# Where ScalarE reads the redo flag: moving a flag load and a branch ahead of the waits for the last stores

## The chip, the cores and the metric

The kernel runs on one core of one Trainium2 chip. Times are device microseconds (us) of that core. The profile's span goes from the first to the last instruction of the program; the device time is about 1.8 us longer.

## The reference, cut to what matters

```python
# x: (1, 384, 384, 384) bfloat16, w1d: (1,) bfloat16
g = jnp.einsum("bhwc->bc", x) / (H * W)      # mean of each channel
s = sigmoid(g * w1d[0])                      # k = 1: one weight
return x * s[:, None, None, :]               # scale each channel
```

The result needs a mean over all of x before the first value may be written. Reading x twice would cost half as much traffic again, so the kernel speculates. It computes a scale `s_early` from the first 135 of 1152 row groups, writes everything with that scale, and meanwhile sums the rest. At the end it computes the true scale, compares the two bit by bit, and repeats the whole pass only if they differ. With these inputs they do not differ.

## The kernel before

SyncE issues the loads of 26 tiles of 4.3 to 4.4 MB. TensorE sums them, VectorE multiplies them in place, ScalarE issues the 26 stores. `plan.final` is the list of the stores' semaphores and values.

```python
    # ... after the last tile: true scale, comparison, flag
    plan.op("scalar", lambda e: e.activation(s_true[:], total[:], ACT_F.Sigmoid, ...), ...)
    plan.op("vector", lambda e: e.tensor_tensor(total[:], s_true[:].bitcast(U16),
                                   s_early[:].bitcast(U16), ALU.not_equal), ...)
    plan.op("vector", lambda e: e.reduce_max(wrong[:], total[:], axis=mybir.AxisListType.X), ...)
    plan.op("vector", lambda e: e.tensor_copy(redo[:], wrong[:]), ...)
    checked = (plan.sems["vector"], plan.count["vector"])
    # ... `again` is the plan of the second pass
    stored = nc.alloc_semaphore("stored")

    with nc.Block() as block:

        def second_pass(name, e):
            e.wait_ge(*checked)
            flag = e.value_load(redo[0:1, 0:1], min_val=0, max_val=1)
            with e.If(flag > 0):
                if name != "scalar":
                    e.wait_ge(stored, 1)
                again.emit(name, e)

        # ... sync and vector: plan.emit(name, e); second_pass(name, e)

        @block.scalar
        def _(e):
            plan.emit("scalar", e)
            for token in plan.final:
                e.wait_ge(*token)
            e.sem_inc(stored, 1)
            second_pass("scalar", e)
        # ... tensor and gpsimd: plan.emit alone
```

A second pass must not overwrite output that a store of the first pass is still writing, so `stored` guards it. ScalarE therefore waits for all stores, gives `stored`, and only then loads the flag and branches. (A semaphore is a counter that one instruction raises and another waits for.) The block ends with a barrier: in the trace the last instruction of each other engine in the block, its drain, raises one semaphore; GpSimd waits until all have raised it, and then releases all with another.

## Time and profile before

| | before |
|---|---|
| device time, median of 3 runs (range) | 533.75 us (533.66 to 533.89) |
| span of the profiled run, which is not one of the three and took 534.2 us | 532.4 us |
| traffic | 113.25 MB read, 113.25 MB written |

These are the span line, the slices of the DMA engines, two queue lines and the total of the traffic from the page of the kernel before. One digit stands for a fortieth of the span; 9 means busy for 90% or more. A queue line gives packets, megabytes and the share of the 16 engines' time.

```profile
span 532.4 us, 2500 instructions
...
DMA  9999999999999999999999999999999999999995
...
q10 hardware_dynamic: 3746, 113.25, 49.3%
...
q14 instruction: 2, 0.02, 0.0%
...
HBM read 113.25 MB, written 113.25 MB: 425 GB/s over the span
```

The kernel is bound by the DMA engines in every slice but the last. There traffic runs out, and an instruction's latency can be seen in the time.

The chain of waits does not show that latency. It ends as follows (start in us, length in us, what):

```profile
504.64 0.57 DVE total L281
505.21 0.02 issue
505.24 0.56 DVE wrong L289
505.80 0.02 issue
505.82 0.15 DVE redo L295
```

The chain stops at 505.97 us, 26.4 us before the span's end, because it follows the engines' own work. After that there are only DMA transfers and instructions of the sequencers: waits, register loads, branches. The view of one source line shows these too. Below are lines 326 (flag load), 327 (branch), 346 (store waits), 347 (last wait with the increment) and 322 (closing drain and barrier) of before. "SPq" is SyncE's sequencer, the part of the engine that waits and branches; ACT is ScalarE, DVE VectorE and POOL GpSimd; after the count come minimum, median and maximum duration in ns, then the start of the first and of the last one in us.

```profile
L326 SPq TENSOR_LOAD <-redo x1: 832/832/832, 506.0 to 506.0; - x1
L326 DVEq TENSOR_LOAD <-redo x1: 932/932/932, 506.0 to 506.0; - x1
...
L326 ACTq TENSOR_LOAD <-redo x1: 475/475/475, 530.9 to 530.9; - x1
L326 ACTq FUSED_REGOPS  x1: 173/173/173, 531.4 to 531.4; - x1
L326 ACTq SEQ_ASSERT  x1: 18/18/18, 531.6 to 531.6; - x1
...
L327 ACTq COMPARE_BRANCH  x1: 54/54/54, 531.6 to 531.6; - x1
...
L346 ACTq EVENT_SEMAPHORE  x12: 38/38/38, 504.0 to 530.7; - x12
...
L347 ACTq EVENT_SEMAPHORE  x1: 38/38/38, 530.8 to 530.8; - x1
...
L322 POOLq EVENT_SEMAPHORE  x2: 17/17/17, 532.2 to 532.3; - x2
...
L322 SPq DRAIN  x1: 51/51/51, 507.7 to 507.7; - x1
...
L322 ACTq DRAIN  x1: 67/67/67, 532.1 to 532.1; - x1
```

SyncE and VectorE loaded the flag at 506.0 us; SyncE was in its drain at 507.7. ScalarE loaded it at 530.9. Its drain at 532.1 is what the barrier waited for. The same records with three decimals, for ScalarE and the barrier (start, duration, what; us):

```
530.712 0.038  ScalarE  wait that the last store ended (its 16th landing: 530.691)
530.789 0.038  ScalarE  wait (already met) and increment of `stored`
530.893 0.475  ScalarE  load of the flag
531.397 0.173  ScalarE  register operations
531.600 0.018  ScalarE  assert
531.647 0.054  ScalarE  compare and branch (taken)
532.135 0.067  ScalarE  drain
532.234 0.017  GpSimd   barrier: all have drained
532.312 0.017  GpSimd   barrier: release; the span ends at 532.417
```

I call the time from the start of the first of these lines to the span's end the **tail**: here 532.417 - 530.712 = 1.705 us. The start of a wait's record may be used as the moment at which the store was seen: the Trainium skill, "Perfetto Trace Analysis", section "Per-engine timelines", says that for an instruction run by the sequencer the profiler reports as start the moment when all its semaphores are satisfied. This trace agrees: the wait's record starts 21 ns after the last landing.

### The profile page before, as it was taken

Reading aid. Unit: us, or ns where it says so; the run is one execution under the profiler, and the core shown is the slowest. Engines: PE = TensorE matmul, PEld = TensorE weight load, DVE = VectorE, ACT = ScalarE, POOL = GpSimd, SP = SyncE. Lnnn points to the kernel's source line nnn. Section 1 sums busy time; section 2 is a strip of 40 time slices with the busy share of each in tenths; the row PEclk is TensorE's granted clock in tenths of the full one; section 3 lists DMA queues with packets and bytes.
Section 4 is the critical chain, followed back from the end, with each engine's and each line's share of the span. In section 5 each row is a group of like instructions: output and inputs, shape, how many; then the busy total and the mean of one; then the engine's idle time right before and its main releaser. Section 6 shows DMA issues by size and latency. Waiting matters only on the chain.

```text
span 532.4 us, 2500 instructions
## 1 busy us (share of the span) xinstructions
PE 243.2 (46%) x1153; PEld 127.8 (24%) x1153; DVE 236.7 (44%) x34; ACT 2.7 (1%) x4; POOL 0.3 (0%) x5
## 2 busy tenths in 40 slices
PE   0979643347156156266266156266265255165100
PEld 0435311123023033133133033033132133032000
DVE  0006999551642642633633642632633642633700
ACT  1000000000000000000000000000000000000000
POOL 0000000000000000000000000000000000000000
PEclk9989867587686786775676686786675686786755
DMA  9999999999999999999999999999999999999995
GB/s 371 418 450 421 411 415 454 418 449 417 447 416 449 414 448 425 434 442 423 432 444 424 432 443 421 434 444 415 439 444 421 434 440 424 434 442 423 432 440 241
DMA packets 7501, 226.66 MB, mean 426 GB/s; under 512 B 834, under 2 KB 834, under 8 KB 834
## 3 DMA queue, kind: packets, MB, share of 16 engines
q1 hardware_dynamic: 3744, 113.25, 49.6%
q10 hardware_dynamic: 3746, 113.25, 49.3%
q8 instruction: 9, 0.15, 0.1%
q14 instruction: 2, 0.02, 0.0%
HBM read 113.25 MB, written 113.25 MB: 425 GB/s over the span
## 4 chain that ended last, share of the span: by engine, by line
another core or an unknown queue 63%; DMA 20%; DVE 7%; PE 3%; SPq 1%; issue 1%; ACT 0%; DVEq 0%
DMA arena<-in_x_dram 12%; DMA out_dram<-arena 8%; DVE arena L165 7%; PE acc L206 3%; SPq L91 1%; ACT s_early L255 0%; ACT s_true L273 0%; DVE total L281 0%; DVE total L249 0%; DVE wrong L289 0%; DVE total L267 0%; SPq L99 0%; DVE redo L295 0%; DVEq L99 0%
## 5 line engine op out<-in xcount | busy, mean ns | idle before, releaser
L206 PE MATMUL acc<-arena,ones 128*128 128x384 bf16 x1152 | 243.0, 383 | 249.2 <-DMA arena<-in_x_dram 249.2
L165 DVE TENSOR_TENSOR arena<-arena,s_early 128x16896 bf16<-128x16896 bf16 (+1 forms) x26 | 234.1, 9019 | 224.3 <-PE acc L206 223.6
L206 PEld LDWEIGHTS acc<-arena,ones 128*128 128x128 bf16 x1152 | 127.7, 113 | 364.2 <-DMA arena<-in_x_dram 258.9
L249 DVE COPY total<-acc 128x384 f32<-128x384 f32 x1 | 0.6, 558 | 42.1 <-PE acc L206 42.1
L273 ACT ACTIVATE s_true<-total,w_scaled 128x384 bf16<-128x384 f32 x1 | 0.6, 615 | 458.2 <-DVE total L267 458.2
L177 ACT ACT_TABLE_LOAD x1 | 1.3, 1283 | 1.3 <-PEq L370 1.3
L183 PE MATMUL acc<-w_one,ones 1*128 1x1 bf16 x1 | 0.2, 158 | 2.0 <-DMA w_one<-in_w1d_dram 2.0
L281 DVE TENSOR_TENSOR total<-s_true,s_early 128x384 f32<-128x384 uint16 x1 | 0.6, 559 | 0.7 <-ACT s_true L273 0.7
L255 ACT ACTIVATE s_early<-total,w_scaled 128x384 bf16<-128x384 f32 x1 | 0.6, 616 | 42.4 <-DVE total L249 42.4
L192 DVE TENSOR_SCALAR w_scaled<-acc 128x1 f32<-128x1 f32 x2 | 0.2, 153 | 1.2 <-PE acc L183 1.2
L183 PEld LDWEIGHTS acc<-w_one,ones 1*128 1x128 bf16 x1 | 0.1, 99 | 2.0 <-issue 2.0
L289 DVE TENSOR_REDUCE wrong<-total 128x1 f32<-128x384 f32 x1 | 0.6, 553 | 0.0
L267 DVE TENSOR_TENSOR total<-total,acc 128x384 f32<-128x384 f32 x1 | 0.5, 546 | 0.0
L173 DVE MEMSET ones<- 128x128 bf16 x1 | 0.2, 165 | 0.8 <-PEq L370 0.8
L177 ACT ACTIVATE warm<-warm 128x1 f32<-128x1 f32 x1 | 0.2, 203 | 0.0
L295 DVE CAST redo<-wrong 128x1 int32<-128x1 f32 x1 | 0.2, 154 | 0.0
L370 POOL MEMSET const-bfloat16-1.0<- 128x1 bf16 x1 | 0.1, 102 | 0.0
L370 POOL MEMSET const-uint8-127<- 128x1 uint8 x1 | 0.1, 102 | 0.0
L172 POOL MEMSET warm<- 128x1 f32 x1 | 0.1, 99 | 0.3 <-POOLq L370 0.3
L370 POOL MEMSET const-float32-0.0<- 128x1 f32 x1 | 0.1, 99 | 0.2 <-issue 0.2
L370 POOL MEMSET const-float32-1.0<- 128x1 f32 x1 | 0.1, 99 | 0.0
## 6 DMA issues: line engine op xcount, KB each, us to landing
arena<-in_x_dram SPq DMA_DIRECT2D x18, 4224.0 KB, 28.9
out_dram<-arena ACTq DMA_DIRECT2D x18, 4224.0 KB, 72.2
arena<-in_x_dram SPq DMA_DIRECT2D x8, 4320.0 KB, 31.0
out_dram<-arena ACTq DMA_DIRECT2D x8, 4320.0 KB, 58.7
w_one<-in_w1d_dram ACTq DMA_DIRECT2D x1, 0.0 KB
```

Of the source, the lines that this page charges most:

```text
L91: ("op", lambda e: e.dma_start(out, in_), self.pool[i], 16)
L165: return lambda e: e.tensor_tensor(v, v, s_b, ALU.mult)
L177: lambda e: e.activation(warm[:, 1:2], warm[:, 0:1], ACT_F.Sigmoid),
L183: lambda e: e.matmul(acc[2][:, 0:1], ones[0:1, :], w_one[0:1, 0:1], start=True, stop=True),
L206: lambda e, i=i: e.matmul(acc[bank][:, :C], ones[:], at(place + i, 1), start=first and i == 0, stop=last and i == n - 1,),
L249: lambda e: e.tensor_copy(total[:], acc[0][:, :C]),
L255: lambda e: e.activation(s_early[:], total[:], ACT_F.Sigmoid, scale=w_scaled[:, 0:1]),
L267: lambda e: e.tensor_tensor(total[:], total[:], acc[1][:, :C], ALU.add),
L273: lambda e: e.activation(s_true[:], total[:], ACT_F.Sigmoid, scale=w_scaled[:, 1:2]),
L281: lambda e: e.tensor_tensor(total[:], s_true[:].bitcast(U16), s_early[:].bitcast(U16), ALU.not_equal),
L289: lambda e: e.reduce_max(wrong[:], total[:], axis=mybir.AxisListType.X),
L370: nc = _bacc.Bacc("TRN2", target_bir_lowering=False, num_devices=1)
```

## The change

The intent is that ScalarE loads the flag and branches while the last stores are still under way. In the common case the waits follow the branch. In the rare case they stand in the branch's body, before `stored`.

```diff
             with e.If(flag > 0):
-                if name != "scalar":
+                if name == "scalar":
+                    for token in plan.final:
+                        e.wait_ge(*token)
+                    e.sem_inc(stored, 1)
+                else:
                     e.wait_ge(stored, 1)
                 again.emit(name, e)
 # ...
         @block.scalar
         def _(e):
             plan.emit("scalar", e)
+            second_pass("scalar", e)
             for token in plan.final:
                 e.wait_ge(*token)
-            e.sem_inc(stored, 1)
-            second_pass("scalar", e)
```

## The prediction

> **What bounds the kernel now.** The DMA engines. The page's slices show DMA 9 or more in all but the last, 426 GB/s mean, 113.25 MB read and 113.25 MB written; PE is busy 46%, VectorE 44%, ScalarE 1%. The span is 532.4 us; the device time is 533.75 us. The change touches none of this traffic: only ScalarE's order after its last store is issued.
>
> **The tail, from the raw instruction records** (the page does not count these instructions as busy, so its chain of waits hides them):
> - 503.53 us: ScalarE issues the last store; 503.99: it computes s_true.
> - 505.98: VectorE has written redo. SyncE and VectorE load the flag at once (0.83 and 0.93 us, beside full DMA traffic), branch, and sit in the closing drain at 507.66 and 507.95.
> - ScalarE meanwhile walks through its store waits, two to an instruction, 77 ns apart when already met. The last store lands at 530.69; its wait is done at 530.75, and the last pair with the increment at 530.83.
> - Only then: flag load 530.893 (0.475 us), register operations 531.397 (0.173), assert 531.600, compare-and-branch 531.647 (0.054), and a gap of 0.43 us until its drain at 532.135. The barrier then ends at 532.417.
>
> So 530.87 to 532.135, about 1.26 us, is serial work behind the last store, and every other engine is waiting for it.
>
> **What the change moves.** Load, register operations, branch and the jump's gap go before the final waits. I expect them from 506.0 to about 507.7, slower than at the tail because DMA is busy, but with 23 us of slack before the last store lands. The nine already met waits then run after the branch, to about 508.4; the three that really wait still end at 510.8, 520.8 and 530.7. After the last pair (530.83) ScalarE goes directly to its drain at about 530.88. Nothing is added to the path that is taken: the waits in the body are jumped over, the increment disappears. The body grows by some 13 instructions, so the jump is a little longer. The Trainium skill, "Runtime: NRT & Kernel Launch", section "Instruction fetch mechanics", says that a taken branch whose target lies outside the two-page window stalls for a fetch; in before none of the three taken branches shows such a stall (gaps of 0.43, 0.45 and 0.16 us), and if the longer body caused one, it would fall into the slack.
>
> Each taken branch seems to be followed by one 8 KB instruction fetch: two at 511.0 and 511.2 (SyncE, VectorE), one at 532.75, after the span's end. ScalarE's would move to about 511. If the close of the program waits for that last fetch (ended 533.13), the device time gains up to about 0.6 us more than the span; I give this a third.
>
> **Prediction.** Span 532.4 - 1.26 = 531.15 us. Device time 532.4 us (about -0.25%), 8 in 10 between 531.6 and 532.9. Faster by over 2%: 0.01; within 2%: 0.98; slower by over 2%: 0.01.
>
> **What would show it.** Right: ScalarE's flag load near 506 us; its branch before its waits; the last semaphore wait within about 0.1 us of the drain; span shorter by 1.2 to 1.3 us; issue times of loads and stores unchanged. The fetch at the very end gone would show the second part. Wrong: an unconditional branch or another jump gap of about 0.4 us between last wait and drain; a fetch stall after the last wait.
>
> **What would make it wrong.** The last store's landing differs between executions by more than the effect; the compiler arranges blocks so that the waits stand elsewhere or a jump follows them; the changed code shifts instruction fetch at the start or end of the program; the extra fetch gain is larger than thought.

## The result, and the profile after

| | before | after |
|---|---|---|
| device time, median of 6 runs (range) | 533.81 us (533.46 to 535.01) | 532.63 us (532.25 to 532.91) |
| span of the profiled run | 532.4 us | 530.9 us |
| tail of the profiled run | 1.705 us | 0.465 us |

The ratio is 0.9975, with a 95% interval of 0.9962 to 0.9988. A ratio is the mean time of one kernel's runs over that of the other's of the same rounds, so it is not quite the ratio of the medians in the table. One run of before, 535.01 us, stands 1.1 us above the other five; without it the ratio of the means would be 0.9979, near the 0.9976 and 0.9978 of the repeats below.

The page of the kernel after, for the lines shown of before:

```profile
span 530.9 us, 2501 instructions
...
DMA  9999999999999999999999999999999999999996
...
q10 hardware_dynamic: 3746, 113.25, 49.5%
...
q14 instruction: 3, 0.02, 0.0%
...
HBM read 113.25 MB, written 113.25 MB: 427 GB/s over the span
```

The traffic is the same. One more instruction fetch lies within the span. The chain of waits ends with the same instructions, and again says nothing about the tail:

```profile
502.29 0.57 DVE total L281
502.86 0.02 issue
502.88 0.56 DVE wrong L289
503.44 0.02 issue
503.47 0.15 DVE redo L295
```

The sequencers' lines of after; the store waits are now line 351:

```profile
L326 SPq TENSOR_LOAD <-redo x1: 830/830/830, 503.6 to 503.6; - x1
L326 ACTq TENSOR_LOAD <-redo x1: 868/868/868, 503.7 to 503.7; - x1
L326 DVEq TENSOR_LOAD <-redo x1: 923/923/923, 503.7 to 503.7; - x1
...
L326 ACTq FUSED_REGOPS  x1: 173/173/173, 504.6 to 504.6; - x1
...
L327 ACTq COMPARE_BRANCH  x1: 54/54/54, 504.8 to 504.8; - x1
...
L351 ACTq EVENT_SEMAPHORE  x13: 17/38/38, 505.3 to 530.4; - x13
...
L322 POOLq EVENT_SEMAPHORE  x2: 17/17/17, 530.7 to 530.8; - x2
...
L322 ACTq COMPARE_BRANCH  x1: 38/38/38, 530.5 to 530.5; - x1
L322 ACTq DRAIN  x1: 8/8/8, 530.7 to 530.7; - x1
```

ScalarE's flag load now stands beside those of SyncE and VectorE. It takes 0.868 us there in place of 0.475, and costs nothing, because the last store lands some 27 us later. The end, with three decimals:

```
530.409 0.038  ScalarE  wait that the last store ended
530.486 0.038  ScalarE  branch to the end of the block, which carries the last wait (already met)
530.651 0.008  ScalarE  drain
530.692 0.017  GpSimd   barrier: all have drained
530.770 0.017  GpSimd   barrier: release; the span ends at 530.874
```

From the last real wait to the drain it takes 0.242 us in place of 1.423 us. Together with a drain that is shorter by 0.06 us, the tail shrank by 1.705 - 0.465 = 1.240 us.

The two profiled spans differ by 1.54 us, though, because the last wait was also over 0.30 us earlier in this run (530.409 against 530.712). That part is scatter between executions: in the nine further profiles of kernels with the same traffic below, that moment lies anywhere from 530.05 to 531.20 us. Nor is the last store's issue a measure: it came 2.36 us earlier in after (501.17 against 503.53), and its landing only 0.30 us earlier. From 500 to 525 us the DMA engines of both runs are busy all the time (share 0.99 to 1.02). Over the eleven profiles of the table below the last store is issued between 501.07 and 504.25 us with no clear relation to the last wait: 501.07 goes with 530.32 (e4), 504.25 with 530.56 (e1).

### The profile page after: what moved, and what is told of

Read it like the earlier page. It is cut to its first block, busy times and chain, and to the rows that moved or that the text cites. A ratio compares the mean times of both kernels' runs of the same rounds, so it can differ in the third digit from the quotient of the medians.

```text
span 530.9 us, 2501 instructions
## 1 busy us (share of the span) xinstructions
PE 241.9 (46%) x1153; PEld 127.3 (24%) x1153; DVE 236.8 (45%) x34; ACT 2.7 (1%) x4; POOL 0.3 (0%) x5
## 4 chain that ended last, share of the span: by engine, by line
another core or an unknown queue 63%; DMA 19%; DVE 7%; PE 3%; SPq 1%; issue 1%; ACT 0%; DVEq 0%
DMA arena<-in_x_dram 12%; DMA out_dram<-arena 8%; DVE arena L165 7%; PE acc L206 3%; SPq L91 1%; ACT s_true L273 0%; ACT s_early L255 0%; DVE total L281 0%; DVE total L249 0%; DVE wrong L289 0%; DVE total L267 0%; SPq L99 0%; DVE redo L295 0%; DVEq L99 0%
```

## The experiments

Three theories were tested.

1. The gain is the serial latency of flag load, register operations, branch and jump behind the last store.
2. The gain comes from instruction fetch. In before, an 8 KB fetch started at 532.75 us, 0.33 us after the span's end. In after there is none there, and three lie at 508.5 to 509.1 us, where before had two at 511.0 and 511.2. They look like one fetch for each engine that jumped (the record doesn't name the engine): e4_no_check, where ScalarE has no branch, shows only two. But e8_after_flag_set, where no engine jumped there, still shows one, at 510.5 us, so this is a guess. The end of the program might have waited for the late one.
3. The stores landed earlier for another reason.

There are three groups, each on one chip: e1, e2, e4 and e5; then e3, e5b, e6 and e7; then e8, e9 and e10. Each kernel ran 5 times (e8 and e9 once) beside 9 runs of before on the same chip. Here are all of the tails, read from the profiled runs:

| kernel | last store wait starts | drain starts | span ends | tail | ratio to before (95%) |
|---|---|---|---|---|---|
| before | 530.712 | 532.135 | 532.417 | 1.705 | 1 |
| after | 530.409 | 530.651 | 530.874 | 0.465 | 0.9975 (0.9962 to 0.9988) |
| e5_after_again | 530.406 | 530.648 | 530.871 | 0.465 | 0.9976 (0.9963 to 0.9990) |
| e5b_after_third | 530.051 | 530.292 | 530.516 | 0.465 | 0.9978 (0.9964 to 0.9992) |
| e1_load_first | 530.556 | 531.206 | 531.499 | 0.943 | 0.9986 (0.9972 to 0.9999) |
| e2_before_two_loads | 530.116 | 532.058 | 532.350 | 2.234 | 1.0009 (0.9996 to 1.0023) |
| e3_after_two_loads | 530.090 | 530.328 | 530.551 | 0.461 | 0.9977 (0.9963 to 0.9990) |
| e4_no_check | 530.318 | 530.497 | 530.720 | 0.402 | 0.9973 (0.9960 to 0.9987) |
| e6_gpsimd_waits | 530.325 | 530.518 | 530.786 | 0.461 | 0.9977 (0.9964 to 0.9991) |
| e7_waits_after_block | 530.891 | none | 530.929 | 0.038 | 0.9958 (0.9945 to 0.9972) |
| e10_after_block_again | 531.202 | none | 531.240 | 0.038 | 0.9961 (0.9948 to 0.9975) |

The starts scatter by over 1 us between profiles, more than some of the gains. The tails repeat to some ns (the changed kernel's three are all 0.465 us, those of e7 and e10 both 0.038; the others were profiled once), so they carry the attribution; the ratios tell whether the device time follows.

### e1_load_first: the load early, the branch late

```diff
             flag = e.value_load(redo[0:1, 0:1], min_val=0, max_val=1)
+            if name == "scalar":
+                for token in plan.final:
+                    e.wait_ge(*token)
+                e.sem_inc(stored, 1)
             with e.If(flag > 0):
 # ... (and these three lines are gone from the end of ScalarE's first pass)
```

> The kernel before with the flag load, its register operations and its assert ahead of ScalarE's store waits; the branch stays behind them. Theory 1 (the gain is the serial latency of load, register operations, branch and jump gap behind the last store, 1.24 us in the trace, less the jump that the changed kernel gained): the load's part, 530.893 to about 531.65 in the trace of before, is 0.75 us, so from the start of the last real store wait to the span's end 1.70 - 0.75 = 0.95 us, and the device time 0.7 us less than before (ratio 0.9986). Theory 2 (what counts is that the jump's instruction fetch no longer falls at the end of the program): the branch is still last, so no gain, ratio 1.000. Theory 3 (the stores landed earlier, the order at the end is not the cause): tail as in before, 1.7 us.

The tail was 0.943 us, and the device time 532.83 us median against 533.62 us of before. ScalarE's lines 326, 330 (last wait with the increment), 331 (branch) and 322 of this kernel:

```profile
L326 ACTq TENSOR_LOAD <-redo x1: 817/817/817, 506.7 to 506.7; - x1
...
L330 ACTq EVENT_SEMAPHORE  x1: 38/38/38, 530.6 to 530.6; - x1
...
L331 ACTq COMPARE_BRANCH  x1: 54/54/54, 530.7 to 530.7; - x1
...
L322 ACTq DRAIN  x1: 78/78/78, 531.2 to 531.2; - x1
```

The load is early, and the branch is still behind the waits; with three decimals it starts at 530.730, and the drain at 531.206. The load with its register work was worth 1.705 - 0.943 = 0.762 us. The rest of the change was worth 0.943 - 0.465 = 0.478 us: 0.41 us for the branch and its jump less the new jump at the end, and 0.07 us because the drain is shorter (0.078 and 0.008 us). The late fetch after the branch is present here (531.82 us), and the gain came all the same; that speaks against theory 2, and the tail against theory 3.

### e2_before_two_loads: one more load in the tail

```diff
             flag = e.value_load(redo[0:1, 0:1], min_val=0, max_val=1)
+            if name == "scalar":
+                flag = e.value_load(redo[0:1, 0:1], min_val=0, max_val=1)
```

> The kernel before, but ScalarE loads the flag twice, both behind the last store. Theory 1: one more load costs its own 0.475 + 0.173 us and gaps, 0.7 us: tail 2.4 us, device time 0.7 us more, ratio 1.0013. Theories 2 and 3: the branch and its fetch, and the stores' landing, are unchanged, so ratio 1.000.

The tail was 2.234 us, 0.529 us more than before. The device time rose by 0.59 us (medians 534.21 and 533.62); the ratio's interval just includes 1. The direction is that of theory 1; my size was a third too large (0.7 us). The two loads, lines 326 and 328 of this kernel, show why:

```profile
L326 ACTq TENSOR_LOAD <-redo x1: 477/477/477, 530.3 to 530.3; - x1
...
L328 ACTq TENSOR_LOAD <-redo x1: 286/286/286, 531.0 to 531.0; - x1
```

The second load took 286 ns, not 475. What makes the first one dearer these runs do not separate: only the first stands right behind semaphore waits and carries one itself.

### e3_after_two_loads: the same second load, early

The edit is that of e2, in the changed kernel.

> The changed kernel, but ScalarE loads the flag twice, both ahead of its store waits. Theory 1: both loads end some 22 us before the last store lands, so the second one, which costs 0.7 us or a little more beside the DMA traffic, is free: tail 0.465 us and ratio to before the same as the changed kernel's, 0.9977. A rival, that each flag load costs the same wherever it stands (by traffic or by the engine's issue): 0.7 us given back, ratio 0.999.

The tail was 0.461 us and the ratio 0.9977, the same as the changed kernel's in its group (0.9978). The second load took 592 ns at 506.2 us. A flag load costs about half a microsecond behind the last store and nothing ahead of it.

### e4_no_check: no flag and no branch on ScalarE

```diff
             e.sem_inc(stored, 1)
-            second_pass("scalar", e)
```

If the flag were set, this kernel would give a wrong result; it serves only as a bound.

> The kernel before without any second pass on ScalarE (it would give a wrong result if the flag were set; it is not for these inputs). Theory 1: all of load and branch goes and no jump is added between the last wait and the drain, so the tail from the start of the last real store wait is 0.35 us or less, against 1.70 before and 0.465 in the changed kernel; the device time 1.3 to 1.4 us less than before, ratio 0.9975. Theory 2: the fetch after ScalarE's branch goes as well, so the same; it says nothing of more gain than the changed kernel has. Theory 3: no gain beyond noise.

The tail was 0.402 us, a little more than the 0.35 us that I had expected: the last pair of waits, the drain and the barrier alone take that long. The changed kernel pays only 0.063 us more. That is the price of the branch that leads from the end of its waits to the block's end: from wait to drain 0.242 us, and here 0.179 us. The rest of the check is hidden.

### e5_after_again and e5b_after_third: the changed kernel beside the others

No edit.

> The changed kernel itself, for comparison with the others on one chip. Theory 1: tail 0.465 us as before in its trace, device time 1.2 to 1.3 us below before, ratio 0.9977; the difference of device time and span is the same in both, about 1.8 us, so nothing is gained after the span. Theory 2: the difference of device time and span is smaller than in before.

> The changed kernel once more, on the chip of this group, so that the other three have it beside them: tail 0.465 us, ratio 0.9977.

The tail was 0.465 us in both. Device time less span, averaged over all runs of a kernel, settles theory 2:

| | device time, mean | span, mean | difference |
|---|---|---|---|
| before, group of e5 | 533.67 us | 531.87 us | 1.80 us |
| e5_after_again | 532.46 us | 530.64 us | 1.82 us |
| before, group of e5b | 533.76 us | 531.97 us | 1.79 us |
| e5b_after_third | 532.55 us | 530.68 us | 1.87 us |

The late fetch is gone from after, and the time after the span is no shorter. The packed trace also holds the updates of semaphores, which no view prints. In e1_load_first, which has the late fetch, and in e5_after_again, which has not, the work that closes the program begins a sweep of updates over nearly all semaphores 0.68 us after the span's end and makes its last update 1.91 us after it. Theory 2 falls. The spans differ by 1.23 us and 1.29 us, which is the tails' 1.24 us within the scatter. Nothing is left for theory 3.

### e6_gpsimd_waits: another engine waits for the stores

```diff
             with e.If(flag > 0):
-                if name != "scalar":
-                    e.wait_ge(stored, 1)
+                e.wait_ge(stored, 1)
                 again.emit(name, e)
 # ... (ScalarE: no waits and no increment after plan.emit)
         @block.gpsimd
         def _(e):
             plan.emit("gpsimd", e)
+            for token in plan.final:
+                e.wait_ge(*token)
+            e.sem_inc(stored, 1)
```

> A version that may beat both: GpSimd, which has nothing else to do and runs the closing barrier, waits for the stores and gives the increment; ScalarE loads the flag, branches and drains early, its body waits for the increment as the other engines' do. Theory 1: no branch follows the last wait and ScalarE's own drain and its hop to GpSimd go, so the tail is 0.25 to 0.40 us against 0.465, a gain of 0.1 to 0.2 us on the changed kernel (ratio to before 0.9974). If GpSimd's sequencer is slower with waits or its own drain (0.17 us at the start of the trace) comes behind them: tail 0.5 us, no gain.

The tail was 0.461 us: no gain. GpSimd's drain and barrier lines (322) of this kernel:

```profile
L322 POOLq EVENT_SEMAPHORE  x2: 17/17/17, 530.6 to 530.7; - x2
...
L322 POOLq DRAIN  x1: 41/41/41, 530.5 to 530.5; - x1
```

ScalarE's branch and its drain are out of the way. But GpSimd now puts a drain of its own between the last wait and the barrier, and its barrier step starts 0.278 us after the last real wait, where in the changed kernel it is 0.283 us. One small step was traded for another.

### e7_waits_after_block and e10_after_block_again: the waits behind the closing barrier

The diff is against the changed kernel.

```diff
             second_pass("scalar", e)
-            for token in plan.final:
-                e.wait_ge(*token)
 # ... (after the block)
+    for token in plan.final:
+        nc.scalar.wait_ge(*token)
```

> A version that may beat both: ScalarE's waits for the last stores stand behind the closing barrier, so that drain and barrier too run while the last stores are under way. Theory 1 carried to its end: only the last wait itself remains, tail about 0.12 us against 0.465, device time 0.3 us below the changed kernel, ratio to before 0.997. If the program's close needs a chain of its own behind the last instruction that the barrier had overlapped, the span shrinks but the device time does not.

> The version with the waits behind the closing barrier once more, on another chip, because its first five runs spread over 1.3 us. If its gain on the changed kernel is real: ratio to before 0.9957 to 0.9967, device time less span about 1.47 us where the others have 1.8, and tail 0.04 to 0.12 us. If it was the stores' landing by luck: the ratio nearer 0.997, as the shorter tail alone gives.

Lines 360 (store waits) and 322 of e7_waits_after_block:

```profile
L360 ACTq EVENT_SEMAPHORE  x13: 38/38/38, 507.5 to 530.9; - x13
...
L322 POOLq EVENT_SEMAPHORE  x2: 17/17/17, 507.3 to 507.4; - x2
```

The barrier is over at 507.5 us, and the last wait is the last instruction of the program. The tail is 0.038 us. The time after the span shrank too: the mean difference of device time and span is 1.47 us in e7 and 1.49 us in e10, where their groups' runs of before have 1.79 and 1.85 us. The records of semaphore updates show where it went. Behind the program stand nine updates of semaphore 2, which the program does not use, and the sweep over the semaphores. In before and in after all nine lie 0.24 to 0.76 us after the span's end, and the sweep begins 0.68 us after it. In e7 the first of the nine stands at 507.76 us, right behind the barrier, the other eight lie 0.12 to 0.44 us after the span's end, and the sweep begins 0.35 us after it; e10 repeats this. So the first step of the close no longer waits for the stores, and the rest starts 0.33 us earlier. In e7's group the mean device time was 531.71 us against 532.55 us of the changed kernel, 0.84 us less: 0.44 us of it within the span (means 530.24 and 530.68 us, and the tails differ by 0.427 us) and 0.40 us behind it (1.47 and 1.87 us). I had expected 0.3 us, because I had thought only of the tail. This version beats before in two groups on two chips. Beside the changed kernel it ran in one group only; there it is 0.2% ahead (0.9958 against 0.9978), but its runs spread over 1.3 us and the intervals of the two ratios overlap. That it is ahead rests on the tail and the time after the span, which both repeat in e10.

### e8_after_flag_set and e9_after_block_flag_set: is the rare case still right?

```diff
-                w_scaled[:, i : i + 1], acc[2][:, 0:1], 1.0 / float(P * n)
+                w_scaled[:, i : i + 1], acc[2][:, 0:1], (1.0e5 if i == 0 else 1.0) / float(P * n)
```

This spoils the early scale, so the kernel's own comparison sets the flag. It is applied to the changed kernel (e8) and to the version with the waits behind the barrier (e9).

> The changed kernel with the scale of the early sigmoid made 100000 times too large, so that the first pass writes wrong values and the flag is set by the kernel's own comparison. It tells whether the waits inside the branch's body do their work: the output must be correct by the second pass. The second pass reads and writes everything again and starts only after the last store has landed, so about 531 us more: 1060 to 1075 us. If the new order let the second pass start early or hang, the result would be wrong or never come.

> The version with the waits behind the closing barrier, with the same spoiled early scale: correct by the second pass, and the same 1060 to 1075 us.

Both gave the correct result, in 1060.92 us and 1060.11 us (one run each). In e8 the increment of `stored` started at 529.618 us, and SyncE's first load of the second pass was issued at 529.680 us: the waits in the body did hold it back. This run also shows the branch that is not taken: the next instruction starts 0.04 us after the branch's record ends. After the taken branch it is 0.42 us in after (504.855 to 505.279) and 0.43 us in before. The jump at the end of after's waits (line 322) is shorter: 0.13 us from its record's end to the drain.

## Why the prediction was right

**Time.** I predicted 532.4 us with 531.6 to 532.9; it was 532.63 us. The predicted change was -0.25%, and the measured ratio is 0.9975. That the two agree to the last digit is partly luck: without the one slowest run of before it would be 0.9979, and 533.75 - 1.26 would have been 532.5 us.

**What bounds the kernel, and where the slack lies: right.** The traffic and its rate did not change, and ScalarE's load and branch found their place some 25 us before the last landing. That the load is slower beside the traffic (0.868 us) was as expected, and e3 shows that even a second one is free there.

**The sum of the tail: right in total.** I had 1.26 us; it was 1.24 us. e1 splits it into 0.76 us for the load and its register work and 0.48 us for the rest. That the total fits so well is luck in part, because two terms were missing and cancel: the new branch costs 0.063 us, and ScalarE's drain became 0.059 us shorter.

**"After the last pair (530.83) ScalarE goes directly to its drain": wrong, and small.** The changed kernel has a branch there which carries the last wait. It costs 0.063 us against a kernel without it (e4). I had named this risk, at 0.4 us.

**The late instruction fetch, one third likely to give up to 0.6 us more: did not come true.** The fetch moved as foreseen, but the time after the span stayed at 1.8 us (e5, e5b). The Trainium skill, "Runtime: NRT & Kernel Launch", section "Instruction fetch mechanics", says that a taken branch to a target outside the two-page window stalls for a fetch. No run here shows such a stall: after the three taken branches of after the next instructions start at 505.28, 505.28 and 505.56 us, and the first of the fetches only at 508.50 us.

**"Issue times of loads and stores unchanged": a poor mark.** The last store was issued 2.36 us earlier in the profile of after, by scatter (the same kernel issued it at 502.74 and 503.18 us in e5 and e5b), and the landing hardly moved. "Span shorter by 1.2 to 1.3 us" was likewise too fine for one pair of profiles (1.54 us); averaged over the runs of a group it was 1.23 and 1.29 us.

## What to carry to other kernels

When a kernel is bound by DMA, look at what the sequencers do behind the last landing; the groups and the chain of waits leave it out, and the lines of single instructions show it. A flag load, a branch, a drain or a barrier that does not need the last store belongs ahead of the wait for it: here each of them cost its full latency behind the wait and nothing ahead of it. For such small effects compare the tail within each profile, which repeats to some ns, and use the device times, over several runs, only to confirm it.

## What the Trainium skill lacked or had wrong

- "Advanced Engine Details and Errata", section "Control Flow Timing", gives a compare-and-branch about 108 ns and does not say whether it is taken. From the start of ScalarE's branch to the start of the next instruction it is 0.09 us here if the branch is not taken (e8, e9), near that figure, but 0.47 to 0.49 us if it is. VectorE's taken branch needs 0.23 us; why it is shorter, no run shows.
- "Runtime: NRT & Kernel Launch", section "Instruction fetch mechanics", gives about 200 ns per register for a register load, which the page describes as a load from HBM; that section has no figure for a load from SBUF, the core's on-chip memory, where the flag lies. Here such a load took 286 ns right after another one, 475 ns as the first one behind the last store, and 0.75 to 0.93 us as the first one beside full DMA traffic.
- That section warns of the stall after a taken branch. It gives no figure for a taken branch without a stall (0.47 to 0.49 us on ScalarE here), nor does it say that a fetch which follows it need not hold anything up: the fetch at 532.75 us of before could go without any gain after the span.
- No page says that a program's own closing barrier delays the work behind the program. Waiting for the stores behind it took 0.43 us from the span and 0.3 to 0.4 us from the time after the span (1.47 and 1.49 us in place of 1.8 to 1.9 us).
